# Attention into two MLPs on one core: stores of the first MLP issued by GpSimd, two kinds of loads issued earlier, TensorE in source order

## The chip, the cores and the metric

The kernel runs on one core of a Trainium2 chip. Times are device microseconds (us) of one execution, from its start to its end. The core's engines are called by the names of the profile: PE is TensorE (matmul), DVE is VectorE, ACT is ScalarE, POOL is GpSimd, and SP is SyncE, which in this kernel issues DMAs and computes nothing. "SPq" and "POOLq" are the instruction queues of SP and GpSimd, in which a DMA issue has a start and a duration like any other instruction. The granted clock is the share of TensorE's full clock that the chip allowed in a stretch.

## The reference

Three computations follow each other. `x` has shape 8 x 8 x 512 x 64 (batch, head, position, width), `state` 8 x 8 x 32 x 64.

```
a     = softmax(x @ state^T / 8)          # per batch and head: 512 x 32
xread = a @ state
a2    = softmax(state @ x^T / 8)          # 32 x 512
sread = a2 @ x
t     = concat([xread, sread], positions) # per batch 544 rows of 8*64 = 512
h = t @ w_in ; g = h if h >= 1, 0 if h <= -1, else (h+1)^2/4 ; t = g @ w_out
h = t @ w2_in; g = max(h,0) + alpha*min(h,0)                 ; out = g @ w2_out
```

The two MLPs have 4352 rows of 512 and an inner width of 2048. All is float32.

## The kernel before, in words

**Number form.** For the MLPs each float32 operand is split into a high part (a cast by ACT, `hi_`, line 73) and a low part (the difference, by DVE, `lo_`, line 76), and each product is three matmuls, high x high, high x low, low x high (`mm3`, line 84, and line 584). The weights of the two MLPs arrive as 64-bit words and are decoded to float32 by ACT and DVE (`dec0`, `dec1`).

**First MLP and attention, one loop.** The 4352 rows are worked off in nine tiles: tile t is 512 positions of batch t for t = 0 to 7, and tile 8 holds the 256 rows that come from `sread` of all batches. A step is a pair (t, f) of a tile and one of 16 slices of the inner width; `gi(t, f)` is its number, 16t + f. Step i issues the first product of step i+2 (`h_mm`, six matmuls, tile `hA`), the activation of step i+2 (`act_fn`: ACT twice into `y`, then DVE into `g`), the split of step i+1 (`g_split`: `gh` by ACT, `gl` by DVE) and the second product of step i (`out_mm`, twelve matmuls into four accumulators `accA`). After the last slice of a tile the accumulators are copied to `oA` and stored to a DRAM buffer `xd`.

**Work beside the loop.** In the steps of tile b-1 the attention of batch b is computed in stages `s0` to `s9`, for two halves q of four heads each. `ld_x1` (line 119) loads x for the scores: for b = 1 one DMA, for the other batches eight DMAs of 64 KB for each half (line 130) into two 2 KB buffers of the pool `up` (`U`, 72 buffers). `ld_x2` loads x a second time for `sread` into a 4 KB buffer of the pool `vp` (`V`, 14 buffers).

**V.** The first product doesn't use `xread` itself: `xread @ w_in` is the attention weights times `state @ w_in`, and this last product is called V here. `vg_mm` (PE, line 460, tile `vgp`) computes V in two groups g of four batches, for four blocks of the inner width; group 0 is batches 1 to 4, group 1 is batch 0 and 5 to 7. ACT copies it to `vgo` (line 463), `vg_store` (line 473) writes it to the DRAM buffer `vd`, and `vr_load` (line 477, the DMA stands on line 481) reads back, for each batch, block and half, the part that the batch needs (tile `vr`, 128 x 512). `vr_hi` casts it (ACT, tile `vwXYZh` for batch X, block Y, half Z) and `vr_lo` takes the difference. Parts for batch 0 are moved from `vgo` by GpSimd's own DMAs instead (`v0_move`, line 471).

**Weights for the later stages.** `wi_store` (line 422) stores the decoded `w_in` in DRAM for tile 8. For the second MLP, which uses seven products per 2 x 2 block, the weights are combined during tiles 2 to 8: GpSimd makes four sums of each of eight blocks q (`four_sums`, line 628; tiles `sao`, `sbo` for the output weights, `saa`, `sba` for the input weights), `put` splits them (ACT and DVE, tiles `wo`, `wu`), and `put_store` (line 648, DMA on line 650) writes them to `w2d` and `w1d`. `w2_plan` places all this, one key each 3.4 steps from step gi(2, 4) on.

**What sets the order.** All this is put into a table of steps by `at(step, function)` (beside the products of that step) and `by(step, function)` (behind them). The Tile framework's scheduler then sets the order of the instructions on each engine's queue from its own model; each queue is worked off strictly in order. `ld` is SP: all loads and stores named above are issued there, except `v0_move` (GpSimd) and the stores of `oA` (ACT). The second MLP (`second`, from line 890 on) is not touched by the change.

Of the kernel before, what the change touches and what calls it, by code (L numbers as in the profile page):

```python
# [40 lines left out]
def kernel_body(ctx: ExitStack, tc: tile.TileContext, x, state, w1i, w1o, w2i, w2o, alpha, out):  # L41
# [9 lines left out]
    def U(name, dt=F32):  # L51
        return up.tile([128, 512], dt, tag="u", name=name)

    def V(name, dt=F32):
        return vp.tile([128, 1024], dt, tag="v", name=name)
# [7 lines left out]
    act, dve, pool, pe, ld = nc.scalar, nc.vector, nc.gpsimd, nc.tensor, nc.sync  # L63

    def run(*calls):


        gens = [g for g in (fn(*a) for fn, *a in calls) if g is not None]
        while gens:
            gens = [g for g in gens if next(g, gens) is not gens]  # L70
# [23 lines left out]
    vd = [[dp.tile([NH, 128 - 32 * g, 512], F32, name=f"vd{g}_{k}") for k in range(4)] for g in range(2)]  # L94
# [3 lines left out]
    wd = [dp.tile([DM, 512], F32, name=f"wd{k}") for k in range(4)]  # L98
# [4 lines left out]
    A = {}  # L103
# [12 lines left out]
            op=ALU.mult)  # L116
        BD[b] = f

    def ld_x1(b, q):
        A[b, q] = {}  # L120
        if b == 1:
            t = A[b, q]["x1"] = V(f"x1_{b}{q}")
            ld.dma_start(out=t, in_=x[b, 4 * q:4 * q + 4].rearrange("h (s r) d -> (h s) (r d)", r=16))
            return
        A[b, q]["x1"] = [U(f"x1_{b}{q}{u}") for u in range(2)]
        for u, t in enumerate(A[b, q]["x1"]):
            for h in range(2):
                for e in range(2):
                    p = 64 * (h ^ q) + 32 * e
                    ld.dma_start(out=t[p:p + 32].rearrange("s (r i) -> s r i", i=32),  # L130
                                 in_=x[b, 4 * q + 2 * u + h, :, 32 * e:32 * e + 32].rearrange("(r s) i -> s r i", s=32))

    def ld_x2(b, q):
# [8 lines left out]
    def s0(b, q):  # L142
        a = A[b, q]
        x1 = a.pop("x1")
        a["xt"] = []
        for e in range(2):
            t = U(f"xt{b}{q}{e}")
            if b == 1:
                dve.transpose(out=t.rearrange("p (s r) -> p r s", r=16),
                              in_=x1.rearrange("p (r e i) -> p r e i", e=2, i=32)[:, :, e, :])  # L150
            else:
                dve.transpose(out=t, in_=x1[e])
            a["xt"].append(t)
            yield

# [185 lines left out]
    def first_back(q):  # L341
# [4 lines left out]
        a["at"] = ps  # L346

    STAGES = [s0, None, s2, s3, s4, s5, s6, s7, s8, s9]

    W = {}  # L350
    VW = {}
    ST = {}
    G = {}
# [66 lines left out]
        d_load(("wi", blk, c), w1i[c * 128:(c + 1) * 128, blk * 512:(blk + 1) * 512])  # L420

    def wi_store(blk, c):
        ld.dma_start(out=wd[blk][c * 128:(c + 1) * 128, :], in_=G["dec", ("wi", blk, c)])

    def vdirect(b, blk):
        for q in range(2):
# [45 lines left out]

    def vg_store(g, blk, c):
        for h in (2 * c, 2 * c + 1):
            ld.dma_start(out=vd[g][blk][h], in_=G.pop(("vgo", g, blk, h))[32 * g:])

    def vr_load(b, blk, q):
        g = 0 if b < 5 else 1
# [35 lines left out]
    steps = [(t, f) for t in range(NB + 1) for f in range(NF)]  # L514

    def gi(t, f):
        return t * NF + f
# [129 lines left out]

    def put_store(name):
        for dst, src in PQ.pop(name):
            ld.dma_start(out=dst, in_=src)  # L650

    def w1_sums(q):
        r0, r1 = [WR.pop((q, kh)) for kh in range(2)]
# [233 lines left out]
    def late_sums():  # L887
        for kh in range(2):
            key = ("w2i", 7, kh)
            dec0(key)  # L890
            yield
            yield from dec1(key)
            w2i_take(7, kh)
        w1_sums(7)
        yield
        yield from w1_put(7, 0)
        for k in range(1, 4):
            yield from w1_put(7, k)
            put_store(f"wu7{k - 1}")
        yield  # L900
        yield
        put_store("wu73")
# [5 lines left out]
    def second():  # L908


        ahead = 6
        ev = []
        for s in range(NSUP):
            os = [("o", s, n // 8, n % 8) for n in range(56)]
            hs = [("h", s, q, p) for q, p in LS]
            if s:
                ev += [hs[0], back[0], hs[1], back[1], hs[2], back[2], hs[3], back[3]]
            ev += hs[4 if s else 0:-2]
            back = os[-4:]
            ev += [os[0], os[1], hs[-2], os[2], os[3], hs[-1]] + os[4:52 if s + 1 < NSUP else 56]  # L920
        loads, need = [], []
        for n, (kind, s, a, b) in enumerate(ev):
            if kind == "h":
                loads.append((w1_get, s, a, b))
                need.append(n)
            elif kind == "o" and b % 4 < 2:
                for k in range(2):
                    loads.append((w2_get, s, a, b // 4 * 4 + b % 4 * 2 + k))
                    need.append(n + k)
        nl = 6  # L930
        late = late_sums()
        for n, (kind, s, a, b) in enumerate(ev):
            G["unit"] = n
            out_store(n)
            while nl < len(loads) and need[nl] <= n + ahead:
                fn, *arg = loads[nl]
                fn(*arg)
                nl += 1
            if kind == "h":
                h_item(s, a, b)  # L940
                h_after(s, a, b)
                next(late, None)
                if b == 3:
                    o_split(s, 0, a)
                if b == 6 and a in (1, 3, 4, 6):
                    k = (a - 1) // 2 + a // 4
                    o_split(s, 1, k)
                    g_comb(k, 4)
            else:
                m = 8 * a + b  # L950
                if 12 <= m + 5 < 56:
                    o_split(s, *divmod(m + 5, 8))
                if 8 <= m < 12:
                    g_comb(m - 4, 4)
                if 23 <= m < 31:
                    g_comb(m - 23, 1)
                if s + 1 < NSUP and 4 <= m < 8:
                    xr_load(s + 1, m % 2, m // 6)
                o_item(s, a, b % 4 // 2, [b // 4 * 4 + b % 2 * 2 + k for k in range(2)])
                if s + 1 < NSUP and m in XAT:  # L960
                    fn, arg = XSTEPS[XAT.index(m)]
                    fn(s + 1, arg)
        out_store(END + 10)


    side = defaultdict(list)
# [3 lines left out]
    def at(i, fn, *a):  # L970
        side[i].append((fn, *a))

    def by(i, fn, *a):
        behind[i].append((fn, *a))
# [31 lines left out]
    for b in range(1, NB):  # L1006
        t0 = gi(b - 1, 0)
        for q in range(2):
            o = t0 + 4 * q
            n = o if b == 1 else t0 + q - 1  # L1010
            at(n - 2 - (b > 1), ld_x1, b, q)
            at(o + 3, ld_x2, b, q)
            for k, s in enumerate(STAGES):
                if s is s2 and b > 1:
                    if q:
                        at(t0 + 2, s2_all, b)
                elif s:
                    at((n if k == 0 else t0 + q if k == 3 and b > 1 else o) + k, s, b, q)
        for blk in range(4):
            for q in range(2):  # L1020
                o = t0 + 10 + 4 * blk + q
                at(o - 2, vr_load, b, blk, q)
                at(o, vr_hi, b, blk, q)
                at(o + 1, vr_lo, b, blk, q)

# [4 lines left out]
    for blk in range(4):  # L1030
        for c in range(4):
            if blk:
                o = 4 * blk + 1 + c
                at(o, vg_mm, 0, blk, c)
                at(o + 2, vg_store, 0, blk, c)
                o = gi(1, c) if blk < 2 else 4 * blk - 7 + c
                by(o, vg_mm, 1, blk, c)
                if blk > 1:
                    by(o, v0_move, blk, c)
                    if c % 2:  # L1040
                        by(o + 1, vr_hi, 0, blk, c // 2)
                        by(o + 1, vr_lo, 0, blk, c // 2)
                at(o + 2, vg_store, 1, blk, c)
            at(gi(1, 4 * blk + c - 4), wi_store, blk, c)

    for blk in (1, 2, 3):
        for c in range(4):
            o = 4 * blk - 7 + c - (blk > 1)
# [3 lines left out]
    for f in range(1, NF):  # L1052
        o = f - 2 - (f >= NAT)
        at(o - 3, d_load, ("w1o", f), src_w1o(f))
        decode(("w1o", f), o)
    for f in range(NF):
        o = gi(1, f - 3) if f < NAT else f - 2
# [73 lines left out]
    st_build(0)  # L1131
    st_build(1)
    run((s9, 0, 0), (s9, 0, 1), (dec1, ("w1o", 0)))
    for i in range(min(side), len(steps)):
        todo = [(g_split, i + 1)] if 0 <= i + 1 < len(steps) else []
        if i in (-4, -3):
            h_mm(i + 4)
            todo.append((act_fn, i + 4))
        todo += side.pop(i, [])
        if 0 <= i < len(steps) - 2:  # L1140
            h_mm(i + 2)
            todo.append((act_fn, i + 2))
        run(*todo)
        if i >= 0:
            out_mm(i)
        run(*behind.pop(i, []))
    second()


# [27 lines left out]
```

## Time and profile before

| | us |
|---|---|
| median of 3 runs | 1371.51 |
| their range | 1370.38 to 1373.39 |
| the profiled execution, its own time | 1371.31 |
| its span, first to last instruction | 1369.4 |
| PE busy in the span | 1336.7 (98%) |
| DVE busy | 1024.9 (75%) |
| ACT busy | 779.2 (57%) |
| GpSimd busy | 75.2 (5%) |
| mean granted clock | 0.998 |

The profiled execution's time is its span and 1.9 us around it. A busy share is an average over the whole span. PE counts as busy also while a matmul runs at a lower clock, or while one that it has begun is held up, so that lost time can hide in its busy time; a comparison of stretches with equal work shows it. The profile's timeline lists runs of like instructions in order of start; the bracket at a row's end is the time for which the engine stood idle before the row, and what ended this wait.

### The profile page before, as it was taken

The numbers are of one execution on the slowest core, as the hardware profiler recorded it, in microseconds if no ns is written. First come the engines' busy times: TensorE is split into PE (matmuls) and PEld (weight loads), VectorE is DVE, ScalarE is ACT, GpSimd is POOL, SyncE is SP. The second block draws the span as 40 slices with busy tenths as digits, with TensorE's granted clock in tenths as the row PEclk, the third lists the DMA queues.
The fourth block names the chain that finished last, engine by engine and source line by source line (L and its number), as shares of the span: only waits on it lengthen the run. The fifth ranks groups of instructions, "written<-read, shape, count | busy, mean of one in ns | idle before, by whom it ended". The sixth has DMA issues, their size and how long they took to land.

```text
span 1369.4 us, 20766 instructions
## 1 busy us (share of the span) xinstructions
PE 1336.7 (98%) x6936; PEld 1108.2 (81%) x6936; DVE 1024.9 (75%) x1849; ACT 779.2 (57%) x1500; POOL 75.2 (5%) x94
## 2 busy tenths in 40 slices
PE   6999999999999999999999999999999999999998
PEld 3345668787878787888987888888889999999998
DVE  6897464868777877976978796787858777796873
ACT  4667765666666755766665454444635545464552
POOL 0010000011101120211200000000000000000000
PEclk9999999999999999999999999999999999999999
DMA  6978842265585647376467676656687888869875
GB/s 227 339 241 282 221 132 55 70 162 173 146 229 151 194 125 196 127 244 215 148 223 279 215 277 197 232 155 218 212 258 267 283 286 297 275 239 286 266 263 179
DMA packets 279370, 293.82 MB, mean 215 GB/s; under 512 B 136160, under 2 KB 170208, under 8 KB 279264
## 3 DMA queue, kind: packets, MB, share of 16 engines
q1 hardware_dynamic: 271680, 282.08, 64.8%
q10 hardware_dynamic: 7072, 9.37, 2.1%
q0 software_dynamic: 512, 1.05, 0.3%
q8 instruction: 55, 0.90, 0.3%
q14 instruction: 51, 0.42, 0.1%
HBM read 224.53 MB, written 66.06 MB: 212 GB/s over the span
## 4 chain that ended last, share of the span: by engine, by line
PE 85%; DVE 6%; DMA 5%; ACT 2%; issue 1%; SPq 0%; ACTq 0%; DVEq 0%
PE accB L825 24%; PE hB L750 22%; PE accA L584 21%; PE hA L84 12%; DMA vr<-vd 3%; PE vgp L460 2%; PE accA L576 1%; DMA xr<-xd 1%; PE sr L252 1%; DVE g L552 1%; DMA w1d<-wu 1%; DMA wr_wi<-in_moe_w_in_dram 0%; PE et L203 0%; DMA st<-in_state_dram 0%; DVE c L759 0%
## 5 line engine op out<-in xcount | busy, mean ns | idle before, releaser
L825 PE MATMUL accB<-gs,wv 128*128 128x384 f32 (+1 forms) x1680 | 332.1, 356 | 0.9 <-ACT o L843 0.9
L825 PEld LDWEIGHTS accB<-gs,wv 128*128 128x128 f32 x1680 | 300.9, 188 | 27.5 <-ACT o L843 1.6
L750 PE MATMUL hB<-xh,wu 128*128 128x384 f32 (+1 forms) x1120 | 315.6, 357 | 2.8 <-DVE m L759 1.2
L750 PEld LDWEIGHTS hB<-xh,wu 128*128 128x128 f32 x1120 | 205.7, 188 | 23.6 <-ACT p L776 2.2
L750 PE MATMUL hB<-xl,wu 128*128 128x384 f32 (+1 forms) x560 | 199.6, 356 | 0.0
L73 ACT CAST gs<-c 128x384 fp32r<-128x384 f32 (+1 forms) x200 | 109.3, 557 | 76.3 <-PE accB L825 55.8
L552 DVE SCALAR_TENSOR_TENSOR g<-y,hA 128x512 f32<-128x512 f32 (+1 forms) x144 | 93.6, 650 | 67.1 <-ACT y L550 66.7
L757 ACT ACTIVATE m<-c 128x384 f32<-128x384 f32 (+1 forms) x120 | 68.2, 568 | 118.7 <-DVE c L772 109.3
L76 DVE TENSOR_TENSOR gl<-g,gh 128x512 fp32r<-128x512 f32 (+1 forms) x135 | 93.9, 695 | 47.5 <-ACT gh L73 46.7
L549 ACT ACTIVATE y<-hA 128x512 f32<-128x512 f32 (+1 forms) x144 | 82.5, 573 | 69.2 <-PE hA L84 69.0
L76 DVE TENSOR_TENSOR gs<-c,gs 128x384 fp32r<-128x384 f32 (+1 forms) x200 | 114.6, 603 | 4.4 <-ACT gs L73 3.7
L759 DVE SCALAR_TENSOR_TENSOR c<-m,beta_sb,c 128x384 f32<-128x384 f32 (+1 forms) x120 | 80.9, 674 | 46.5 <-ACT m L757 44.1
L750 PEld LDWEIGHTS hB<-xl,wu 128*128 128x128 f32 x560 | 105.1, 188 | 8.7
L73 ACT CAST gh<-g 128x512 fp32r<-128x512 f32 (+1 forms) x135 | 80.2, 594 | 45.3 <-DVE g L552 37.0
L550 ACT ACTIVATE y<-y 128x512 f32<-128x512 f32 (+1 forms) x144 | 87.5, 608 | 3.8
L799 DVE TENSOR_TENSOR c<-c,c 128x384 f32<-128x384 f32 (+1 forms) x120 | 71.8, 608 | 1.9
L772 DVE TENSOR_TENSOR c<-hB,u 128x384 f32<-128x384 f32 (+1 forms) x80 | 48.5, 606 | 16.5 <-PE hB L750 9.1
L76 DVE TENSOR_TENSOR gs<-m,gs 128x384 fp32r<-128x384 f32 (+1 forms) x80 | 47.1, 608 | 16.4 <-ACT gs L73 16.4
L73 ACT CAST gs<-m 128x384 fp32r<-128x384 f32 (+1 forms) x80 | 43.4, 556 | 24.5 <-PE accB L825 21.1
L463 ACT COPY vgo<-vgp 128x512 f32<-128x512 f32 x64 | 34.8, 588 | 32.2 <-PE vgp L460 31.8
L460 PE MATMUL vgp<-wf_wi,sts 64*128 64x512 f32 x128 | 42.7, 640 | 4.8 <-DVE g L552 3.0
L838 DVE TENSOR_TENSOR c<-accB,o 128x384 f32<-128x384 f32 (+1 forms) x30 | 18.2, 608 | 35.9 <-PE accB L825 28.4
(907 smaller groups left out, 2563.4 us busy)
## 6 DMA issues: line engine op xcount, KB each, us to landing
wu<-w1d SPq DMA_DIRECT2D x280, 256.0 KB
wv<-w2d SPq DMA_DIRECT2D x280, 256.0 KB
vr<-vd SPq DMA_DIRECT2D x56, 256.0 KB
w1d<-wu SPq DMA_DIRECT2D x56, 256.0 KB
w2d<-wo SPq DMA_DIRECT2D x40, 256.0 KB
x<-in_x_dram SPq DMA_DIRECT2D x18, 512.0 KB
wr_wi<-in_moe_w_in_dram SPq DMA_DIRECT2D x16, 512.0 KB
wr_w1o<-in_moe_w_out_dram SPq DMA_DIRECT2D x16, 512.0 KB
```

Of the source, the lines that this page charges most:

```text
L73: act.copy(h, raw)
L76: (eng or dve).tensor_tensor(out=l, in0=raw, in1=h.bitcast(F32), op=ALU.subtract)
L84: pe.matmul(ps, a, b, start=(k == 0), stop=(k == n - 1))
L460: pe.matmul(ps[u], ST[g][rows, c * 128:(c + 1) * 128], w[rows], start=True, stop=True)
L549: act.activation(out=y[:, :n], in_=ps, func=AF.Relu, bias=0.5, scale=0.5)
L550: act.activation(out=y[:, :n], in_=y[:, :n], func=AF.Square)
L552: dve.scalar_tensor_tensor(out=g[:, :n], in0=y[:, :n], scalar=1.0, in1=ps, op0=ALU.min, op1=ALU.max)
L584: pe.matmul(ACC[k][:, :n], a, b, start=(f == 0 and j == 0), stop=(f == NF - 1 and j == 2))
L750: pe.matmul(ps, a[:, kk], b, start=(new and m == 0), stop=(m == 5), skip_group_check=True)
L759: dve.scalar_tensor_tensor(out=g, in0=m, scalar=beta_sb[:, f:f + 1], in1=h, op0=ALU.mult, op1=ALU.add)
L799: dve.tensor_tensor(out=o, in0=x, in1=y, op=op)
L825: pe.matmul(ps, a[:, js], b, start=(new and k == 0 and n == 0), stop=(k == 7 and n == 2), skip_group_check=True)
```

## The change

- `wi_store`, `vg_store` and `put_store` are issued by GpSimd (`pool`) instead of SP: 16, 64 and 128 DMAs.
- `ld_x1` takes one 4 KB buffer of `vp` for each half of batches 2 to 7 instead of two 2 KB buffers of `up`, and is called with one half of the buffer at a time, at steps t0-6+2q+u (t0 is the first step of the tile in which the batch's attention is computed); before, at t0+q-4.
- `vr_load` is placed three steps ahead of its cast instead of two.
- Block 1 of group 1 of `vg_mm` is placed at steps 5 to 8 of tile 1 instead of 0 to 3.
- PE's instructions of steps gi(1,0) to gi(8,-2)-1 keep the order of the source (`manual_schedule`); the scheduler orders the rest as before.

```diff
-    def ld_x1(b, q):
-        A[b, q] = {}
+    def ld_x1(b, q, us=(0, 1)):
+        if 0 in us:
+            A[b, q] = {"x1": V(f"x1_{b}{q}")}
+        t = A[b, q]["x1"]
         if b == 1:
-            t = A[b, q]["x1"] = V(f"x1_{b}{q}")
             ld.dma_start(out=t, in_=x[b, 4 * q:4 * q + 4].rearrange("h (s r) d -> (h s) (r d)", r=16))
             return
-        A[b, q]["x1"] = [U(f"x1_{b}{q}{u}") for u in range(2)]
-        for u, t in enumerate(A[b, q]["x1"]):
+        for u in us:
             for h in range(2):
                 for e in range(2):
                     p = 64 * (h ^ q) + 32 * e
-                    ld.dma_start(out=t[p:p + 32].rearrange("s (r i) -> s r i", i=32),
+                    ld.dma_start(out=t[p:p + 32, u * 512:u * 512 + 512].rearrange("s (r i) -> s r i", i=32),
                                  in_=x[b, 4 * q + 2 * u + h, :, 32 * e:32 * e + 32].rearrange("(r s) i -> s r i", s=32))
...
     def wi_store(blk, c):
-        ld.dma_start(out=wd[blk][c * 128:(c + 1) * 128, :], in_=G["dec", ("wi", blk, c)])
+        pool.dma_start(out=wd[blk][c * 128:(c + 1) * 128, :], in_=G["dec", ("wi", blk, c)])
...
     def vg_store(g, blk, c):
         for h in (2 * c, 2 * c + 1):
-            ld.dma_start(out=vd[g][blk][h], in_=G.pop(("vgo", g, blk, h))[32 * g:])
+            pool.dma_start(out=vd[g][blk][h], in_=G.pop(("vgo", g, blk, h))[32 * g:])
...
     def put_store(name):
         for dst, src in PQ.pop(name):
-            ld.dma_start(out=dst, in_=src)
+            pool.dma_start(out=dst, in_=src)
...
             n = o if b == 1 else t0 + q - 1
-            at(n - 2 - (b > 1), ld_x1, b, q)
+            if b == 1:
+                at(o - 2, ld_x1, b, q)
+            else:
+                for u in range(2):
+                    at(t0 - 6 + 2 * q + u, ld_x1, b, q, (u,))
...
                 o = t0 + 10 + 4 * blk + q
-                at(o - 2, vr_load, b, blk, q)
+                at(o - 3, vr_load, b, blk, q)
...
-                o = gi(1, c) if blk < 2 else 4 * blk - 7 + c
+                o = gi(1, 5 + c) if blk < 2 else 4 * blk - 7 + c
                 by(o, vg_mm, 1, blk, c)
...
-    for i in range(min(side), len(steps)):
+    def step(i):
...
+    for i in range(min(side), gi(1, 0)):
+        step(i)
+    with tc.manual_schedule(engines={mybir.EngineType.PE}):
+        for i in range(gi(1, 0), gi(8, -2)):
+            step(i)
+    for i in range(gi(8, -2), len(steps)):
+        step(i)
```

What the scheduler makes of it is shown at three places. In the rows, names stand as in the program with a number behind; `<-` is read as "from".

SP's queue at the end of tile 3, before. `vr420` and `vr421` are the two halves of block 2 of batch 4's V part, `wo3x` the split output weights of block q = 3, `x2_50` the second load of x for batch 5.

```order
L130 DMA x1_511_3647<-in_x_dram 32x16x32 x4
L650 DMA w2d_90<-wo30_3660 128x512
L650 DMA w2d_90<-wo32_3737 256x1x256 x2
L650 DMA w2d_90<-wo33_3795 256x1x256 x2
L137 DMA x2_50_3914<-in_x_dram 128x16x64
L481 DMA vr420_3784<-vd0_2_82 128x1x512
L357 DMA wr_w2o_10_3922<-in_moe2_w_out_dram 128x512
L481 DMA vr421_3829<-vd0_2_82 128x1x512
```

The same place in SP's queue with the change.

```order
L357 DMA wr_w2o_9_3726<-in_moe2_w_out_dram 128x512
L137 DMA x2_50_3910<-in_x_dram 128x16x64
L357 DMA wr_w2o_10_3918<-in_moe2_w_out_dram 128x512
L481 DMA vr420_3723<-vd0_2_82 128x1x512
L481 DMA vr421_3780<-vd0_2_82 128x1x512
L357 DMA wr_w2o_11_4051<-in_moe2_w_out_dram 128x512
```

The stores of `wo3x` are gone from the queue, the loads of x for batch 5 (`x1_5..`) stand further ahead, and the two V parts follow each other directly.

GpSimd's queue in tile 2 with the change, at block q = 1 of the output weights.

```order
L650 DMA w2d_90<-wo00_2694 128x512
L650 DMA w2d_90<-wo11_3062 256x1x128 x4
L628 TENSOR_TENSOR sao1_2965<-wf_w2o_2_2688,wf_w2o_3_2888 128x4x2x32
L628 TENSOR_TENSOR sbo1_2966<-wf_w2o_2_2688 128x4x2x32
L628 TENSOR_TENSOR sao1_2965<-sao1_2965,wf_w2o_2_2688 128x4x2x32
L628 TENSOR_TENSOR sbo1_2966<-wf_w2o_3_2888,sao1_2965 128x4x2x32
L650 DMA w2d_90<-wo12_3113 256x1x256 x2
L650 DMA w2d_90<-wo13_3158 256x1x256 x2
L650 DMA w2d_90<-wo10_3025 128x512
```

Before, GpSimd's queue held only the four sums of each q here; now nine stores lie among them, and four (those of `wo11`) stand ahead of the sums, as they do for q = 3 and 4.

PE's queue at the start of tile 1, before.

```order
L584 MATMUL accA13_1569<-gh16_1491,w_w1o_0l_1390 128x512
L460 MATMUL vgp110_1582<-wf_wi_1_0_396,sts1_368 128x512
L460 MATMUL vgp111_1583<-wf_wi_1_0_396,sts1_368 128x512
L84 MATMUL hA13_1590<-ath10_1030,vw100h_1166 128x512
```

The same matmuls of `vgp11` with the change.

```order
L584 MATMUL accA13_1571<-gh21_1732,w_w1o_5l_1645 128x512
L460 MATMUL vgp110_1809<-wf_wi_1_0_396,sts1_368 128x512
L460 MATMUL vgp111_1810<-wf_wi_1_0_396,sts1_368 128x512
L84 MATMUL hA18_1817<-ath10_1032,vw120h_1626 128x512
```

They now stand behind the products of step 5 of the tile (`gh21`) and no longer of step 0 (`gh16`).

## Rows read from the trace of the kernel before

**Rows 1.** The page: span, and the busy time of each engine.
```profile
span 1369.4 us, 20766 instructions
PE 1336.7 (98%) x6936; PEld 1108.2 (81%) x6936; DVE 1024.9 (75%) x1849; ACT 779.2 (57%) x1500; POOL 75.2 (5%) x94
```

**Rows 2.** Windows, tiles 1 to 7: length, busy PE, PEld, DVE, ACT, POOL; PEclk, DMA share, GB/s.
```profile
158.39:240.96 82.57, 79.01 (x395) 58.50 (x393) 44.11 (x81) 49.91 (x89) 0.00 (x0) 0.98 0.46 127
240.96:310.07 69.11, 69.11 (x377) 55.78 (x376) 51.78 (x95) 44.33 (x81) 7.08 (x8) 1.00 0.43 117
310.07:379.33 69.26, 69.26 (x377) 55.70 (x376) 57.51 (x106) 44.69 (x85) 8.05 (x8) 1.00 0.59 163
379.33:451.56 72.23, 69.93 (x378) 55.62 (x376) 54.28 (x101) 44.61 (x83) 6.97 (x8) 1.00 0.68 184
451.56:520.69 69.13, 69.13 (x377) 55.72 (x376) 57.42 (x104) 45.18 (x85) 12.04 (x12) 1.00 0.55 156
520.69:593.67 72.98, 70.63 (x377) 55.66 (x376) 57.76 (x107) 46.34 (x88) 7.98 (x8) 1.00 0.61 183
593.67:660.14 66.47, 65.84 (x307) 54.90 (x306) 48.66 (x79) 42.66 (x77) 11.62 (x12) 1.00 0.62 203
```

**Rows 3.** Timeline of PE: `vgp` in tile 0, then in tile 1.
```profile
71.18 1.13 PE L460 MATMUL vgp<-wf_wi,sts 64*128 64x512 f32 x4
72.23 1.98 PE L576 MATMUL accA<-g,wf_w1o 128*128 128x512 f32 x4
...
176.90 1.12 PE L460 MATMUL vgp<-wf_wi,sts 64*128 64x512 f32 x2 [1.10 <-DVE g L552]
...
185.31 1.12 PE L460 MATMUL vgp<-wf_wi,sts 64*128 64x512 f32 x2 [1.91 <-DVE g L552]
```

**Rows 4.** Timeline of ACT in tile 1.
```profile
173.31 0.62 ACT L73 CAST vw120h<-vr 128x512 fp32r<-128x512 f32 x1 [3.01 <-DMA vr<-vd]
...
181.67 0.62 ACT L73 CAST vw121h<-vr 128x512 fp32r<-128x512 f32 x1 [3.02 <-DMA vr<-vd]
...
183.24 0.59 ACT L549 ACTIVATE y<-hA 128x512 f32<-128x512 f32 x1
```

**Rows 5.** Timeline of ACT in tiles 4 and 6.
```profile
392.09 0.62 ACT L73 CAST vw420h<-vr 128x512 fp32r<-128x512 f32 x1 [5.79 <-DMA vr<-vd]
...
532.39 0.62 ACT L73 CAST vw620h<-vr 128x512 fp32r<-128x512 f32 x1 [3.58 <-DMA vr<-vd]
```

**Rows 6.** Timeline of PE in tiles 4 and 6.
```profile
399.98 0.63 PE L203 MATMUL et<-ident,e 128*128 128x128 f32 x4 [1.78 <-DVE g L552]
...
542.07 0.66 PE L203 MATMUL et<-ident,e 128*128 128x128 f32 x4 [2.35 <-ACT e L195]
```

**Rows 7.** Chain of waits, 379 to 408 us: start, length.
```profile
385.46 10.43 DMA vr<-vd
...
400.61 2.77 PE accA L584 x12
403.37 1.36 PE hA L84 x6
```

**Rows 8.** Timeline of SP's queue at the end of tile 3.
```profile
362.35 6.92 SPq L130 DMA_DIRECT2D x<-in_x_dram  x8
...
372.78 3.93 SPq L130 DMA_DIRECT2D x<-in_x_dram  x4
376.81 3.71 SPq L650 DMA_DIRECT2D w2d<-wo  x5
...
381.92 2.83 SPq L481 DMA_DIRECT2D vr<-vd  x1
```

**Rows 9.** DMA issues of line 471: issue ns min/median/max, first and last start; then its waiters.
```profile
L471 POOL DMA_DIRECT2D vr<-vgo x16: 498/498/1417, 57.6 to 117.1; - x16
...
  ACT vw021h L73: 0.8, 1
```

**Rows 10.** Timeline of ACT in tile 3: the longest wait for a sum of GpSimd.
```profile
338.83 0.62 ACT L73 CAST wo<-sao 128x512 fp32r<-128x512 f32 x1 [1.98 <-POOL sao L628]
```

More of the change, by code (lines that the diff above doesn't have):

```diff
@@ L151, in s0 @@
             else:
-                dve.transpose(out=t, in_=x1[e])
+                dve.transpose(out=t, in_=x1[:, e * 512:e * 512 + 512])
             a["xt"].append(t)
```

## The prediction

> **What bounds the kernel now.** I read the page first: PE is busy 1336.7 of 1369.4 us [rows 1]. Idle PE is at most 32.7 us, and what a change can win has to show as a stretch in which PE takes longer than the same work takes elsewhere. So the second view is the windows, cut at the first second-product of each tile. Tiles 1 to 6 carry the same products and one batch of attention each; three of them, tiles 2, 3 and 5, take 69.11 to 69.26 us with PE busy all through [rows 2]. That is the floor. Tile 1 takes 82.57, tile 4 72.23 and tile 6 72.98. Tile 1 has 18 matmuls more than tile 2 (395 against 377), nearly all from four calls of `vg_mm` (four matmuls each); one call takes 72.23 - 71.18 = 1.05 us where nothing holds it [rows 3], so 4.2 us of tile 1 is work. The excess is
>
> - tile 1: 82.57 - 69.11 - 4.2 = 9.3 us, at a granted clock of 0.98 where the floor tiles show 1.00;
> - tile 4: 72.23 - 69.13 = 3.1 us;
> - tile 6: 72.98 - 69.13 = 3.9 us.
>
> Tile 7 (66.47 us, PE idle 0.6) has another make-up, and I leave it out of the sum.
>
> Third, the timelines, to see what PE waits for. In tile 1 it stands before `vgp` for 1.10 and 1.91 us, until DVE has made a `g` [rows 3]; in tiles 4 and 6 before the transposes into `et`, for 1.78 us (DVE's `g`) and 2.35 us (ACT's `e`) [rows 6]. Neither is a slow engine: ACT, in order, stood before them at a cast of a V part whose load had not landed, for 3.01 and 3.02 us in tile 1 [rows 4], 5.79 in tile 4 and 3.58 in tile 6 [rows 5], and the `y` for the next `g` was queued behind that cast (181.67, then `y` at 183.24 [rows 4]).
>
> Last, the chain of waits and SP's queue, to see why the loads are late. In tile 4 the chain names 10.43 us of a V load issued at 385.46 [rows 7]. Its sister, `vr420`, was issued at 381.92, behind a train of issues: eight of x from 362.35, which take 6.92 us, four more of x in 3.93 us, then five stores of `w2d` in 3.71 us [rows 8]. DMA engines are 68% busy in that tile [rows 2], so the transfer itself is slow too.
>
> **The change part by part.**
>
> *V parts three steps ahead, x six.* A step is 69.11/16 = 4.3 us. One more step covers each of the waits of 3.0 and 3.6 us by itself; the 5.79 us of tile 4 needs more, and gets it: the order puts `vr420` behind a load of weights instead of behind the stores of `wo3x`, and the x loads further ahead. So tiles 4 and 6 fall to the floor: -3.1 and -3.9 = **-7.0 us**. Below, the gain is nothing where landing, not issue, is late (second rival). x in one 4 KB buffer instead of two of 2 KB moves the same bytes in the same eight DMAs a half; cost nothing, unless V's 14 buffers, shared with the x loads, decoded weights and the doubled `wo` tiles, come free late. The two x buffers of a batch are held about three steps longer.
>
> *`vgp11` five steps later.* PE had these matmuls in front of the next `hA` in steps 0 to 3, where ACT has V casts, weight casts and copies of `vgo` at once. In steps 5 to 8 it waits for PSUM from older copies; the work, 4.2 us, remains. With the V loads earlier too, I take 8.5 of the 9.3 us: **-8.5 us**. I leave 0.8 because tile 0's accumulators are drained at the same place by ACT with a rearranging copy (line 595), which stays. Bounds: 9.3, and 0 if ACT's row of work is itself too long there.
>
> *208 stores from SP to GpSimd.* SP loses their issue time. GpSimd gains it, and this is the unknown price: the trace has no store from GpSimd, only 16 moves of 32 rows, at 498 ns median [rows 9]. The stores have 128 or 256 rows. If the price is flat it is 0.5 us; if it goes by rows, 0.498 x 256/32 = 4.0 us. I take 1 us, nearer to the flat end, because the measured row is the only one and GpSimd is otherwise idle (75.2 us busy, 5% [rows 1]). Block q of the output weights brings nine stores, 9 us at this price, beside four sums of 7.08/8 = 0.9 us [rows 2], 3.5 us together; blocks come each 2 x 3.4 steps = 29 us. GpSimd keeps up.
>
> What is queued behind the stores matters more than their sum. The four stores of `wo11` now stand ahead of the sums of q = 1 (likewise q = 3 and 4; in most other blocks two or none). ACT's cast of `wo12` from `sao` stands behind the sums, one step after the cast of `wo11`. From that cast to DVE's difference, which the stores need, is some 2.5 us, then four stores at price c, then three sums, 2.7 us: `sao` is ready 5.2 + 4c after the cast, ACT wants it after about 5. So ACT waits some 4c: 2 us at 0.5, 4 at 1, 8 at 2. Before, the longest such wait was 1.98 us [rows 10]. ACT has room: from one `hA` to its second product PE has two more rounds of 12 and 6 matmuls, 2 x (2.77 + 1.36) = 8.2 us [rows 7], and the chain in between is two activations, `g`, cast, difference, five operations of some 0.65 us (0.59 and 0.62 in [rows 4]), 3.3 us with hand-over 3.6. That leaves 4.6 us. At c = 1 nothing reaches PE by itself; for a coincidence with another wait I charge **+1.5 us** over the eight blocks.
>
> In tile 0 the 16 moves of line 471 share GpSimd's queue with the stores of `vgo`; one cast already waited 0.8 us for such a move [rows 9]. With one or two stores of 1 us ahead of each, I charge **+1.0 us** (0 to 3).
>
> A rule of the Trainium skill speaks against this part: "SBUF — State Buffer", section "A bandwidth-pool intuition that's wrong (but worth ruling out)", has a GpSimd-issued DMA of about 620 ns take about 3100 ns beside a DVE copy, since its descriptors can't be written meanwhile. By that page, as an estimate, c would be 3.1 us and the fourth case below would cost 3 x (12.4 - 4.6) + 8 x (6.2 - 4.6) = 36 us: 1393 us. The trace leans the other way: with DVE busy 75% of the span [rows 1], the moves took 498 ns in the median and 1417 at most [rows 9].
>
> *PE in source order.* The matmuls at tile boundaries move by a few places and stay behind operands that are ready well before; I cost it at 0. What hides it is the 8.2 us between `hA` and its second product; without that cover it would cost a matmul group, 1.36 us, for each of seven boundaries, 9.5 us.
>
> **Sum.** -7.0 - 8.5 + 1.5 + 1.0 = -13.0 us against the profiled execution's own 1371.31 us, which stands 0.2 below the median: 1371.5 - 13.0 = **1358.5 us**. A difference under 0.2%, 2.7 us, is about what a measurement of this kernel can't tell from no change.
>
> **The rivals.**
>
> *1. As summed (0.60).* 1355 to 1363: the low end takes all 16.3 us of excess and no charge, the high end charges 3 us in tile 0 and a stall of about 1.5 us more at GpSimd's sums.
>
> *2. Half given back (0.18).* The V loads stay late because landing is slow: the row of 10.43 us [rows 7] is mostly flight, with DMA shares of 0.68 and 0.61 in tiles 4 and 6 (though 0.59 in tile 3, which loses nothing) [rows 2]. Then tiles 4 and 6 keep their 7.0 us, and 1358.5 + 7.0 = 1365.5; range 1363 to 1368.8. Against it: 5.79 us late, with issues moved ahead by a step and by the stores' 3.7 us.
>
> *3. The wait moves (0.09).* The loads don't come earlier, as the buffers of `vp` that SP's loads need are freed only by GpSimd's stores, and an in-order SP holds the V loads back behind them. Tile 1 then gains only what the moved `vgp` frees, the two stalls of 3.0 us [rows 3], and the two charges of 2.5 eat that: 1371.5 - 3.0 + 2.5 = 1371.0, within 0.2%, 1369 to 1374.
>
> *4. GpSimd's issue is the bound (0.13), slower.* The place is the queue of four stores ahead of the sums; the price is 4c - 4.6 us for each of q = 1, 3, 4, and 2c - 4.6 where two stand ahead (about eight blocks of both weights). Without the charge for coincidences the base is 1357; the gain of 14.5 us is used up at 3(4c - 4.6) + 8(2c - 4.6) = 14.5, c = 2.3. At c = 2.5 it is 3 x 5.4 + 8 x 0.4 = 19.4: 1376.4 us; at 4.0 nine stores and the sums need 39.5 us in each 29, and it would be past 1400. For it: rows per DMA grow by four to eight. Against it: [rows 9], the only price seen.
>
> The change does what it says on the queues, as the order shows; only for the x loads could the buffers undo it, which is the third case.
>
> **How the numbers follow.** Cases 1 and 2 are faster, 0.60 + 0.18, less 0.01 for the edge of case 2: 0.77. Case 3 is the same, 0.09 + 0.01 = 0.10. Case 4 gives slower, 0.13. The range 1354 to 1372 holds case 1 (its low end less 1 us, for the 0.6 us of tile 7), case 2 and half of case 3, 0.82 together.
>
> **What would show it.** Right: the casts of `vw` in tiles 1, 4 and 6 show no wait of over 1 us for `vr<-vd`; tiles 4 and 6 last 69 to 70 us, tile 1 74 to 75 with a clock of 1.00; GpSimd's stores take about 1 us each, and `wo<-sao` waits less than 5 us. Wrong: GpSimd's issues last over 2 us, ACT's longest waits name `sao` or `saa`; or V loads are issued earlier and land as late as before; or tile 0 (before 158 us) is longer by over 3 us.

## The result and the profile after

The changed kernel takes 1359.49 us in the median of four runs (1359.17 to 1360.87), the kernel before on the same chip 1370.95 us; the ratio is 0.9915, 95% interval 0.9898 to 0.9932. Forecast were 1358.5 us and a range of 1354 to 1372. The profiled execution took 1359.17 us, 12.1 less than that of before.

The page of the changed kernel, span and busy times, beside [rows 1]:

```profile
span 1356.9 us, 20813 instructions
PE 1332.6 (98%) x6936; PEld 1107.7 (82%) x6936; DVE 1038.8 (77%) x1849; ACT 781.2 (58%) x1500; POOL 200.2 (15%) x302
```

The span is 12.5 us shorter. GpSimd's 208 stores now count as its instructions, 125 us of issuing. The windows by tile, tiles 1 to 7, with the columns of [rows 2]:

```profile
160.23:236.06 75.83, 75.36 (x395) 56.53 (x393) 44.38 (x80) 48.42 (x88) 5.15 (x10) 1.00 0.24 78
236.06:305.17 69.11, 69.11 (x377) 55.77 (x376) 53.21 (x96) 44.71 (x81) 16.43 (x23) 1.00 0.48 132
305.17:374.38 69.21, 69.21 (x377) 55.70 (x376) 60.93 (x106) 44.86 (x84) 21.95 (x29) 1.00 0.60 181
374.38:443.75 69.37, 69.35 (x377) 55.69 (x376) 54.47 (x102) 45.43 (x83) 18.03 (x26) 1.00 0.62 169
443.75:512.86 69.11, 69.11 (x377) 55.77 (x376) 62.54 (x104) 46.12 (x86) 27.03 (x37) 1.00 0.65 188
512.86:582.13 69.27, 69.27 (x377) 55.70 (x376) 58.94 (x105) 46.74 (x87) 16.30 (x22) 1.00 0.46 149
582.13:647.68 65.55, 65.55 (x307) 54.98 (x306) 48.42 (x77) 42.72 (x77) 19.91 (x28) 1.00 0.59 196
```

Where the time came from, tile by tile, with what the prediction had:

| stretch | before | after | difference | forecast |
|---|---|---|---|---|
| up to tile 1 (start of its second product) | 158.39 | 160.23 | +1.8 | +1.0 |
| tile 1 | 82.57 | 75.83 | -6.7 | -8.5 |
| tiles 2, 3, 5 | 207.50 | 207.43 | -0.1 | (see below) |
| tile 4 | 72.23 | 69.37 | -2.9 | -3.1 |
| tile 6 | 72.98 | 69.27 | -3.7 | -3.9 |
| tile 7 | 66.47 | 65.55 | -0.9 | 0 |
| tile 8 and second MLP | 709.26 | 709.22 | 0.0 | 0 |
| charge for GpSimd's sums, no tile named | | | 0 | +1.5 |

Tiles 4 and 6 have fallen to within 0.3 us of the floor, and the waits that kept them from it are gone. ACT's timeline of the changed kernel, the casts of [rows 4, 5]; a row without a bracket means that ACT did not stand idle before it:

```profile
168.78 0.60 ACT L73 CAST vw120h<-vr 128x512 fp32r<-128x512 f32 x1
171.48 0.60 ACT L73 CAST vw121h<-vr 128x512 fp32r<-128x512 f32 x1
...
379.83 0.60 ACT L73 CAST vw420h<-vr 128x512 fp32r<-128x512 f32 x1
...
518.31 0.60 ACT L73 CAST vw620h<-vr 128x512 fp32r<-128x512 f32 x1
```

SP's queue around the load for `vw420`, beside [rows 8]: two V parts are issued together at 360.98, 19 us before the cast at 379.83. Before, the load was issued at 381.92, and the cast came at 392.09.

```profile
351.42 4.89 SPq L357 DMA_DIRECT2D wr_w2o<-in_moe_w_out_dram  x1
360.98 3.61 SPq L481 DMA_DIRECT2D vr<-vd  x2
364.64 0.97 SPq L357 DMA_DIRECT2D wr_w2o<-in_moe_w_out_dram  x1
```

The price that was unknown, from the views of line 475 (stores of 96 or 128 rows), line 650 (128 or 256 rows) and line 471 (the moves of [rows 9], 32 rows); issue ns, min/median/max:

```profile
L475 POOL DMA_DIRECT2D vd<-vgo x64: 512/539/1347, 35.2 to 206.7; - x64
```
```profile
L650 POOL DMA_DIRECT2D w2d<-wo x72: 556/832/1783, 268.0 to 485.1; - x72
```
```profile
L471 POOL DMA_DIRECT2D vr<-vgo x16: 496/503/1807, 62.4 to 120.7; - x16
...
  ACT vw021h L73: 2.4, 1
```

A store from GpSimd holds its queue for 0.54 to 0.83 us in the median. It goes hardly by rows: 32 rows take 0.50, 96 or 128 take 0.54. The wait for the moves in tile 0 rose from 0.8 to 2.4 us.

What the trace of the change can't tell is which of its parts did this, since any of several could have made the V loads early. The experiments take the parts one by one.

### The profile page after: what moved, and what is told of

Same layout as the page of the kernel before. It is cut to its first block, busy times and chain, and to the rows that moved or that the text cites. A ratio compares the mean times of both kernels' runs of the same rounds, so it can differ in the third digit from the quotient of the medians.

```text
span 1356.9 us, 20813 instructions
## 1 busy us (share of the span) xinstructions
PE 1332.6 (98%) x6936; PEld 1107.7 (82%) x6936; DVE 1038.8 (77%) x1849; ACT 781.2 (58%) x1500; POOL 200.2 (15%) x302
## 4 chain that ended last, share of the span: by engine, by line
PE 92%; DVE 3%; DMA 2%; ACT 2%; issue 1%; POOL 0%; ACTq 0%; DVEq 0%; SPq 0%; POOLq 0%
PE accA L584 25%; PE accB L825 24%; PE hB L750 22%; PE hA L84 14%; PE vgp L460 2%; PE accA L576 2%; PE sr L252 1%; DMA wu<-w1d 1%; DMA vr<-vgo 1%; PE et L203 0%; PE sc L179 0%; DMA st<-in_state_dram 0%; ACT vgo L463 0%; DVE c L759 0%; PE vdp L431 0%
## 5 line engine op out<-in xcount | busy, mean ns | idle before, releaser
L650 POOL DMA_DIRECT2D w2d<-wo x72 | 51.1, 885 | 166.6 <-DVE xsf L273 81.4
L650 POOL DMA_DIRECT2D w1d<-wu x56 | 38.2, 780 | 122.6 <-DVE wu L76 92.4
```

The costliest lines, as they stand in the source:

```text
L650: pool.dma_start(out=dst, in_=src)
```

## The experiments

Ratios are to the kernel before, run on the same chip among the others, with 95% intervals. Its medians there were 1374.88 us beside the first four, 1373.61 beside the next four and 1374.71 beside the last, 3 to 4 us above the first measurement, so that times are best read by their ratio and tiles by the profile. First each part of the change was undone by itself.

**All stores back on SP.** Edit, shown for `put_store` and alike in `wi_store` and `vg_store`:

```diff
-            pool.dma_start(out=dst, in_=src)
+            ld.dma_start(out=dst, in_=src)
```

> The changed kernel with all 208 stores back on SP, the rest kept. Theory A (what made the V parts late was SP's queue of stores and x loads together, and each of the cures takes a part): the extra step of lead covers waits of 3 to 3.6 us, not those of 5.8, so tile 4 loses about 1 us again, tile 1 about 2, tile 6 nothing, and tile 0 gets back the 1.8 us that it lost; 1360 to 1361 us. Theory B (the stores alone did it): tiles 4 and 6 lose their 6.6 us again and tile 1 some 3; 1367 to 1370. Theory C (the lead alone did it): tiles 1, 4 and 6 stay at 75.8, 69.4 and 69.3 us, tile 0 gets back its 1.8; 1357 to 1358.

1357.75 us, ratio 0.9883 (0.9862 to 0.9903): theory C. Tiles 2 to 6 all took 69.11 or 69.12 us, tile 1 75.79. Only tile 7 is worse than with the change:

```profile
510.18:579.29 69.11, 69.11 (x377) 55.77 (x376) 55.52 (x105) 46.24 (x87) 7.38 (x8) 1.00 0.51 160
579.29:646.12 66.83, 65.84 (x307) 54.90 (x306) 47.22 (x77) 42.48 (x77) 11.43 (x12) 1.00 0.60 195
```

The two windows are tiles 6 and 7; tile 7 takes 66.83 us against 65.55. DVE waits there for the loads of `xr`, the second MLP's input: 4.87 us here and 5.11 before, 0.42 with the change. So moving the stores gains 1.3 us in tile 7, and nothing elsewhere where the rest of the change is in place: with the stores back on SP tiles 2 to 6 are 0.5 us shorter together, and tile 0 takes 157.93 us against 160.23.

**V's parts two steps ahead again.**

```diff
-                at(o - 3, vr_load, b, blk, q)
+                at(o - 2, vr_load, b, blk, q)
```

> The changed kernel with the V parts loaded two steps ahead again, stores on GpSimd and x early kept. Theory A: with SP's queue free of stores the loads of V are issued at once, 8.6 us ahead of the cast; landing takes some 4 to 10 us in tile 4, so the cast waits 0 to 2 us, less than ACT's room; 1359 to 1361 us. Theory B (the stores alone): no change, 1359.5. Theory C (the lead alone): the waits of 3 to 6 us come back in tiles 1, 4 and 6, 1366 to 1370.

1361.82 us, 0.9915 (0.9895 to 0.9935), the ratio of the change itself: A or B, not C. Tile 4 lost nothing (69.36). Tile 6 lost 1.9 us (71.20), but not through V: in tiles 1 to 7 no cast waits for a V load. ACT waits there for `xst`, a load of rows for tile 8, and the loss stands in the last two steps of the tile; with the change this wait is 1.11 us.

```profile
576.05 0.41 ACT L73 CAST xsh<-xst 128x256 fp32r<-128x256 f32 x1 [5.77 <-DMA xst<-xsf]
```

With stores off SP and x early, two steps are enough for V.

**The moved V products back at steps 0 to 3 of tile 1.**

```diff
-                o = gi(1, 5 + c) if blk < 2 else 4 * blk - 7 + c
+                o = gi(1, c) if blk < 2 else 4 * blk - 7 + c
```

> The changed kernel with block 1 of group 1 of the V products back at steps 0 to 3 of tile 1. If moving them was what freed tile 1 (they stand in front of the next hA while ACT has the most to do), tile 1 grows from 75.8 to 79 to 82 us and the kernel takes 1363 to 1366. If the late V parts were the cause there and the move did nothing, tile 1 stays within 1 us of 75.8 and the kernel within 1359 to 1361.

1359.53 us, 0.9894 (0.9872 to 0.9916); tile 1 took 75.61 us against 75.83. The move did nothing.

**PE ordered by the scheduler again.** The `with tc.manual_schedule` is left out.

> The changed kernel with PE ordered by the scheduler everywhere, as in the kernel before. Costed at nothing in the prediction: 1359 to 1360 us, tiles 1 to 7 as with the change. The rival, that the source order at tile boundaries is worth something (before, two hA matmuls came late and four early at each of seven boundaries): 0.5 us a boundary, 1362 to 1364.

1358.66 us, 0.9889 (0.9867 to 0.9912). Tile 1 took 74.95 us, 0.9 less than in source order; tiles 2 to 7 were equal within 0.1. Neutral, or slightly against the change.

Then each part was put by itself into the kernel before.

**Only the lead of V's parts**, the first line of the second diff reversed.

> The kernel before with one edit: V's parts loaded three steps ahead instead of two. Theory C (the lead alone is enough): tiles 4 and 6 fall from 72.2 and 73.0 to 69.1 to 69.5 us and tile 1 from 82.6 to 75 to 77, 13 us less than before. Theory D (lead, stores off SP and early x each relieve the same queue, so that any two of them are enough but one is not): the 5.8 us wait of tile 4 shrinks to 1 to 2 us and hides in ACT's room, tile 6 falls to the floor, tile 1 keeps 3 to 5 us of its loss; 7 to 10 us less than before.

1360.86 us, 0.9905 (0.9888 to 0.9922), 12.7 us less than before: theory C. One constant has the whole gain of the change (0.9915, and 0.9906 below). Tiles 1 to 4 of this kernel:

```profile
162.00:238.93 76.93, 75.11 (x395) 56.76 (x393) 42.94 (x79) 48.75 (x88) 0.00 (x0) 1.00 0.44 126
238.93:308.27 69.34, 69.34 (x379) 55.97 (x377) 52.04 (x96) 44.45 (x81) 7.08 (x8) 1.00 0.46 117
308.27:377.15 68.88, 68.88 (x376) 55.59 (x375) 57.51 (x106) 45.00 (x84) 7.74 (x8) 1.00 0.60 171
377.15:447.40 70.25, 70.25 (x383) 56.72 (x381) 55.62 (x103) 44.93 (x83) 7.26 (x8) 1.00 0.67 182
```

In tile 4 the 70.25 us hold six matmuls more than usual, since the scheduler's order differs at the boundary; tiles 5 and 6 took 68.66 and 69.64. Over all 56 loads, the only wait of ACT that is left is 0.8 us:

```profile
526.60 0.62 ACT L73 CAST vw621h<-vr 128x512 fp32r<-128x512 f32 x1 [0.80 <-DMA vr<-vd]
```

**Only the stores on GpSimd**, the three edits of the change to `dma_start`.

> The kernel before with one edit: all 208 stores issued by GpSimd. Theory B (SP's stores are what makes the V loads late): tiles 4 and 6 at 69.1 to 69.5 us, tile 1 at 75 to 77, tile 0 longer by 1.8; 11 to 13 us less than before. Theory D: x loads of 7 us in a row still stand ahead of V's, tile 4 or 6 keeps 1 to 3 us and tile 1 2 to 4; 5 to 9 us less. Theory C: nothing gained in tiles 4 and 6, tile 0 longer; 0 to 3 us less.

1371.89 us, 0.9986 (0.9974 to 0.9998), 1.7 us less than before: the number of theory C, but not its picture. Tile 1 fell to 75.53 us, tile 4 to 70.99 and tile 7 to 65.55, but tile 3 rose to 71.62, tile 5 to 70.79 and tile 6 to 74.50. Two V loads were still late (ACT waited 5.85 us for `vw321`, 3.86 for `vw621`), and in tile 6 ACT also waited 6.26 us for `xst`, as with V two steps ahead. In tile 4 something new stands on the path. GpSimd, ACT and PE there:

```profile
388.54 1.38 POOL L650 DMA_DIRECT2D w2d<-wo  x2 [21.56 <-DVE wo L76]
389.69 0.99 POOL L628 TENSOR_TENSOR sao<-wf_w2o,wf_w2o 128x256 f32<-128x256 f32 x1
```
```profile
392.10 0.62 ACT L73 CAST wo<-sao 128x512 fp32r<-128x512 f32 x1 [2.60 <-POOL sao L628]
393.52 0.62 ACT L73 CAST wo<-sbo 128x512 fp32r<-128x512 f32 x1 [0.80 <-POOL sbo L628]
...
396.13 0.69 ACT L195 ACTIVATE e<-sc,nb 128x512 f32<-128x512 f32 x1 [0.82 <-DVE st L189]
```
```profile
396.96 0.66 PE L203 MATMUL et<-ident,e 128*128 128x128 f32 x4 [1.65 <-ACT e L195]
```

Two stores stand ahead of the sums, ACT is idle for 2.60 and 0.80 us at the casts, and after the second of them PE is idle for 1.65 us at the transposes that need `e`: the mechanism of the fourth rival, at a store price of 0.6 us.

**Only x earlier**, with its 4 KB buffer.

> The kernel before with one edit: x for the scores six steps ahead, in one 4 KB buffer a half. Theory D: the V loads of block 2 no longer stand behind x, but behind the w2d stores; tile 4 gains 1 to 3 us, tile 6 1 to 3, tile 1 0 to 3; 3 to 8 us less than before. Theories B and C: no gain, within 2 us of before.

1364.78 us, 0.9933 (0.9917 to 0.9948), 8.8 us less: above D's 3 to 8. Tile 1 took 75.62 us, 7.0 less where D had 0 to 3. Tile 3 rose to 73.40, with a wait of 5.79 us for `vw321`; tiles 4 and 6 stayed at 70.39 and 70.43, with one of 4.09 for `vw421` in tile 4.

**Only the moved V products.**

> The kernel before with one edit: block 1 of group 1 of the V products at steps 5 to 8 of tile 1. As the changed kernel loses nothing without this edit, two readings are left. Late V parts are the cause of tile 1's loss, and the V products in front of hA only the place where it shows: tile 1 stays at 80 us or more, 0 to 3 us less than before. Or the edit is a second cure for the same loss: tile 1 at 75 to 78, 5 to 7 us less; tiles 4 and 6 unchanged in both.

1378.07 us, 1.0030 (1.0018 to 1.0043): slower than before, outside both readings. The profile shows tile 1 at 84.73 us, PE idle 5.02 us before `et`, because ACT waited 4.60 and 4.92 us for `vw120` and `vw121`. By itself the edit harms.

Taken together, more lead is enough by itself (0.9905), and early x and the stores off SP, with the rest of the change, are enough without it (0.9915); stores alone or x alone are not.

Last, a control, two versions and a test of the room behind GpSimd's sums, on one chip.

**The change unaltered.**

> The changed kernel once more, unaltered, as the measure for the other three on the same chip. 0.9915 of the kernel before, as first measured: 1360 to 1363 us. If the 2 us by which the version with its stores on SP was ahead come from another chip and from the clock in tile 0 and not from the stores, it comes out at 0.989, 1358 to 1359.

1360.43 us (1360.08 to 1365.13), 0.9906 (0.9886 to 0.9926). Its tiles agree with the first profile within 0.1 us; only tile 0 differs, 165.18 us against 160.23.

**A version put together.** From the change, `wi_store` and `vg_store` go back to SP and `manual_schedule` goes; `put_store` stays on GpSimd.

> A version put together from the parts: V's parts three steps ahead, x six, the moved V products and the w2d and w1d stores on GpSimd, as in the change; the wd and vd stores (tiles 0 and 1) back on SP, and PE ordered by the scheduler. If the tiles add up: tile 0 as with all stores on SP (156 to 158 us), tile 1 at 75.0, tiles 2 to 6 at 69.1 to 69.4, tile 7 at 65.55: 1355 to 1357 us, 2 to 4 less than the change on the same chip. If GpSimd's stores cost nothing in tile 0 and the difference there is the clock, it is within 1.5 us of the change.

1357.86 us (1357.40 to 1357.99), 0.9878 (0.9857 to 0.9898). It beats the change on the same chip by 2.6 us with ranges that don't meet. Tile 1 took 74.90 us and tile 7 65.55, as added up; tile 0 was 159.55, longer than expected, and the whole lies just above the 1355 to 1357 expected.

**x at its old steps, 4 KB buffers kept.**

```diff
-                for u in range(2):
-                    at(t0 - 6 + 2 * q + u, ld_x1, b, q, (u,))
+                at(t0 + q - 4, ld_x1, b, q)
```

> The changed kernel with x's loads at their old steps (both halves of a buffer at t0+q-4; the 4 KB buffers stay). If the lead of V's parts is enough by itself: tiles 2 to 6 at 69.1 to 69.5 us, the time that of the change within 1.5 us. If x in front of V still matters with the stores gone: tile 4 or 6 loses 1 to 3 us.

1362.70 us (1357.85 to 1363.95), 0.9906 (0.9885 to 0.9927). In tiles 1 to 7 no cast waited for a V load. Tile 2 took 70.64 us, tile 3 69.74, 2 us in all, not in tiles 4 or 6 and not through V. They stand at the boundary of the two tiles, behind a wait for GpSimd's sums, 0.57 us with the change. ACT, then PE:

```profile
303.73 0.62 ACT L73 CAST wo<-sao 128x512 fp32r<-128x512 f32 x1 [3.32 <-POOL sao L628]
```
```profile
306.82 0.50 PE L584 MATMUL accA<-gh,w_w1o_0h 128*128 128x512 f32 x1 [1.38 <-ACT oA L599]
```

The sums came late because on ACT's queue the cast of `wo` ahead of them stands one step later (297.82 us against 293.80 with the change), and ACT did not stand idle before it: it is the scheduler's order, not a wait for x.

**GpSimd's sums 5 us later.**

```diff
-            pool.tensor_tensor(out=o, in0=a, in1=b, op=op)
+            for _ in range(6 if o is s1 else 1):
+                pool.tensor_tensor(out=o, in0=a, in1=b, op=op)
```

> The changed kernel with GpSimd's first sum of each block done six times (the same values), which makes the sums some 5 us later, as four stores of 2.1 us ahead of them would. It tests the room of 4.6 us that the prediction gave ACT behind such a wait. With that room: ACT's waits for sao and saa go from about 2 to 6 or 7 us in most of 15 blocks, PE stalls for 1.5 to 2.5 us in each of 8 to 12 of them, 15 to 25 us more than the change. If the room is 8 us or the scheduler moves the casts out of the way: 0 to 4 us more. If there were no room: 5 us in each, 60 us more.

1393.65 us, 1.0136 (1.0111 to 1.0161), 33 us more than the change. The five sums more took 4.28 us in the block shown below. Tiles 2 to 7 lost 22.5 us (434.1 against 411.6), inside what was expected for them, and what follows them 9.0 more (718.17 us against 709.22), which I had not counted. The scheduler moved some of ACT's casts behind a neighbour. The waits were shorter than expected (ACT waited for `sao` eight times, 32.6 us in all, at most 6.7), so each cost more than the room of 4.6 us allows. The longest, GpSimd, then ACT, DVE and PE:

```profile
395.61 2.77 POOL L651 DMA_DIRECT2D w2d<-wo  x4 [14.58 <-DVE wo L76]
...
399.50 4.28 POOL L629 TENSOR_TENSOR sao<-wf_w2o,wf_w2o 128x256 f32<-128x256 f32 x5
```
```profile
404.62 0.62 ACT L73 CAST wo<-sao 128x512 fp32r<-128x512 f32 x1 [6.71 <-POOL sao L629]
...
408.03 0.69 ACT L195 ACTIVATE e<-sc,nb 128x512 f32<-128x512 f32 x1 [0.83 <-DVE st L189]
```
```profile
405.27 0.69 DVE L76 TENSOR_TENSOR wo<-sao,wo 128x512 fp32r<-128x512 f32 x1 [6.96 <-ACT wo L73]
406.08 0.69 DVE L76 TENSOR_TENSOR wo<-sbo,wo 128x512 fp32r<-128x512 f32 x1
406.69 0.68 DVE L76 TENSOR_TENSOR gl<-g,gh 128x512 fp32r<-128x512 f32 x1
```
```profile
408.86 1.11 PE L203 MATMUL et<-ident,e 128*128 128x128 f32 x4 [4.53 <-ACT e L195]
409.63 0.78 PE L584 MATMUL accA<-gh,w_w1o_4h 128*128 128x512 f32 x1
```

ACT stood for 6.71 us and PE for 4.53: a room of 2.2 us at this place. One wait holds two queues, because DVE's difference of `wo` is stuck behind the cast, and `gl` and the transposition of `sc` into `st` behind that, and by the profile `e` waits for the latter (0.83 us). The program has `e` read `sc` and not `st`; what ties the two I did not settle. The matmul behind the stall takes 0.78 us where 0.39 is usual; the tile's granted clock is 0.96.

## Why the prediction was right, and where its reasons were not

**What bounds.** The floor of 69.11 us and the 16.3 us of excess were right: the change won 13.3 us in tiles 1, 4 and 6, and none of the tiles 1 to 6 fell below the floor. That ACT's casts of late V parts are the cause is shown: the one edit that only makes these loads earlier has the whole gain (0.9905), and its trace has one such wait left, of 0.8 us. Where long waits stay, so does the loss (73.40 us in tile 3 with x alone), and where they grow, tile 1 does (84.73 us with the moved V products alone). A short one can be free: in tile 3 of the kernel before, ACT waited 3.90 us for `vw321`, and the tile still took 69.26.

**V three steps ahead, x six: -7.0 us, measured -6.6** in tiles 4 and 6. The size holds. What the sum did not see is that this term holds tile 1 as well.

**`vgp11` five steps later: -8.5 us. This step failed**, though tile 1 did gain 6.7. Undoing the edit changes tile 1 by 0.2 us; alone, it makes the kernel 0.3% slower. I read PE's stalls before `vgp` [rows 3] as belonging to the place of `vgp`. They were the late casts of [rows 4], seen at the next instruction on PE; the prediction had said so itself and then booked the gain to another edit. Each of three other edits alone, lead, stores or x, brings tile 1 to 75.5 to 76.9 us. The 0.8 us kept for the drain was too little: 2.5 us above floor and work remain (75.83 - 73.3), of which the source order on PE has 0.9.

**Stores at 1 us each: 0.54 to 0.83**, nearer to the flat end, as chosen. The four stores ahead of q = 1's sums took 2.3 us. GpSimd in the changed kernel, and ACT's cast behind it:

```profile
295.44 2.81 POOL L650 DMA_DIRECT2D w2d<-wo  x4 [17.44 <-DVE wo L76]
297.72 1.28 POOL L628 TENSOR_TENSOR sao<-wf_w2o,wf_w2o 128x256 f32<-128x256 f32 x1
```
```profile
300.42 0.62 ACT L73 CAST wo<-sao 128x512 fp32r<-128x512 f32 x1 [0.57 <-POOL sao L628]
```

The wait is 0.57 us, not 4c. By ACT's timeline the cast of `wo11` began at 293.80: the stores followed it by 1.6 us, not 2.5, and ACT came to the next cast after 6 us, not 5. The longest of all is 2.17 us (q = 4), beside 1.98 before [rows 10]; it is 1.99 at q = 2 as well, where no store of its own block stands ahead of the sums, so their count does not set it. The charge of 1.5 us came to at most 0.5, by which tiles 2 to 6 are longer than with the stores on SP.

**The room of 4.6 us** behind such a wait, and with it the fourth rival's point c = 2.3, was wrong on the unsafe side. The two stalls above before `et` give 3.40 - 1.65 = 1.8 and 6.71 - 4.53 = 2.2 us: about 2. I had followed the chain through `y`, `g` and `gl` alone and counted it as if DVE were free; the exponential `e` behind the same wait is needed sooner. The room goes by the place: read in the same way, it is 1.3 us at a tile's end in the kernel with later sums (ACT waited 3.59 us at 310.40, PE 2.34 at 312.59), and 3.5 in the middle of one (5.94 at 344.88, 2.42 at 351.60); none of these places gives 4.6. The change's own waits, up to 2.17 us at one cast and 2.81 at two in a row (tile 5, which stays at 69.11), fit into it, the first of them barely. The rival kept its mechanism and its sign, and a delay of some 4 us costs 33.

**Tile 0: +1.0, measured +1.8 and, in the second profile, +6.8.** The mechanism was right: the cast of `vw021` waits 2.40 and 3.52 us for the moves, where with the `vd` stores on SP it waits 0.8 to 1.3, and PE stalls for 1.4 and 2.5 us (0.5 before); the 3.52 the profile puts down to a store of `vgo` in the same queue. The rest goes with the clock (below), but the two are not separated: with the `vd` stores on SP tile 0 took between 157.86 and 162.00 us in the profiles, so that +1.8 alone shows nothing.

**Tile 7, left out, gained 0.9**: DVE's wait for `xr` falls from 5.11 to 0.42 us. That `xr` comes earlier because no stores stand in front of it on SP's queue fits the run with the stores back on SP, where the wait is 4.87 us.

**The rivals.** Landing was not the cause: loads issued 19 us ahead were in time. That the waits move to buffers was not seen in ACT's casts. By the Trainium skill, "SBUF — State Buffer", section "A bandwidth-pool intuition that's wrong (but worth ruling out)", a store would have taken some 3.1 us beside a DVE copy. The trace does not show it: with DVE busy 77% of the span, the medians were 0.54 and 0.83 us and the longest of these stores 1.78.

So the number came out because the wait that three edits fight was found and sized; which of the edits pays was half guessed wrong. That it is within 1 us is in part luck: tile 1 gained 1.8 us less than forecast, tiles 4 and 6 0.4 less, and tile 0 lost 0.8 more, while the charge of 1.5 us was hardly used and tile 7 gave 0.9 that the sum left out.

## What to carry to other kernels

When an in-order engine waits at a load, ask first for the load's lead in steps: one constant here gave all that five edits gave together. Size a stall where it is caused, not at the instruction in front of which it shows, and book it to one edit only. When computing the room behind a wait, follow every queue that the wait holds up and all that stands in them, not only the main chain; here a second engine and a side branch cut 4.6 us to about 2, and other places gave 1.3 to 3.5.

## What was unexpected on the chip

The granted clock falls to half, the 1.2 GHz level, in tile 0 of some executions and not of others with nearly the same work. Windows of 20 to 30 and 30 to 35 us, with the columns of [rows 2], of the kernel before and of the second profile of the change:

```profile
20.00:30.00 10.00, 6.58 (x92) 2.84 (x92) 9.93 (x26) 5.55 (x13) 0.00 (x0) 1.00 0.86 291
30.00:35.00 5.00, 4.45 (x18) 2.36 (x19) 3.46 (x7) 2.62 (x5) 0.00 (x0) 1.00 0.42 165
```
```profile
20.00:30.00 10.00, 6.44 (x88) 2.50 (x88) 9.93 (x26) 5.16 (x11) 1.92 (x3) 0.83 0.99 382
30.00:35.00 5.00, 4.33 (x15) 2.07 (x13) 3.33 (x6) 1.17 (x2) 0.00 (x0) 0.50 1.02 398
```

PE was busy 6.58 and 6.44 us from 20 to 30 us, nearly alike, and only the second fell, within this window; from 20 to 26 us, with the clock at 1.00 in both, it was busy 4.43 us in each. The first profile of the change fell too (0.50 from 30 to 35 us), and so did the version put together, whose `vd` stores are on SP, so the drop does not hang on GpSimd's stores; of the profiles of all runs only that of the kernel before stayed at 1.00 there. The second profile of the change fell again later, to 0.92 and 0.91 from 90 to 110 us, where the first did not. The clock is thus part of why its tile 0 took 165.18 us and not 160.23; how much of the 4.95 us is the clock and how much the longer wait for the moves is not separated. It is why differences of 2 us between whole kernels here are to be read by tiles.
